# Attention's bias added by VectorE from broadcast rows, softmax factors applied where x is loaded

## The chip, the cores and the metric

One core of a Trainium2 chip runs the whole program. TensorE (PE) multiplies matrices, VectorE (DVE), ScalarE (ACT) and GpSimd (POOL) do the elementwise work, and SyncE (SP) issues the transfers, all of them on one queue. The metric is device time in microseconds, the median of three runs: 1035.31 us before (1035.18 to 1039.88).

## The reference

Attention of 4 batches, 8 heads, 576 tokens and head size 64, with a bias from running sums; then two feed-forward stages over 2304 tokens (width 512; 2048 and 1536 inner columns).

```python
scores = scale * q @ k.T                              # scale = 1/8
cum = np.cumsum(np.maximum(s, 0.0), axis=-1)
bias = -(cum[:, :, :, None] - cum[:, :, None, :])
scores = np.where(causal, -1e9, scores + np.minimum(bias, 0.0))
scores -= scores.max(-1, keepdims=True)
attn = np.exp(scores); attn /= attn.sum(-1, keepdims=True) + 1e-9
x = attn @ v                                          # heads side by side: (2304, 512)
h = x @ w_in; x = (h * np.cos(h)) @ w_out             # FF1, d_ff 2048
# FF2: rms norm, silu(x @ w_gate) * (x @ w_val) @ w_out, d_ff 1536
```

Within a row of scores the term of the query cancels in the softmax, so what a row needs is cum of the key, up to a constant.

## The kernel before

The kernel writes its operations into a list with costs and priorities; a planner then plays a list schedule on five engines and issues the instructions of each engine in the order it found. The times in it are its own; on the chip each engine follows that fixed order and waits on semaphores. Attention's steps get priorities one after the other, `P_ATT` (9000 ns) per pair of heads; a tick of FF1 (256 tokens by 256 inner columns) has priority `T_FF1` + 8094 ns times its number, so from 45 us on in the planner's time attention and FF1 are interleaved on every engine.

Attention runs over 16 pairs of heads (`Run`), four for each batch. A pair has two parts: "a" (query tiles 0 and 1) and "b" (tiles 2, 3 and "p", which puts both heads' last 64 queries into one tile). A unit of a part does the scores, the exponentials, and two units later (`DEPTH`) the transposes of the exponentials and the product with V (`av`); the order is a, then b with tile 2 and p, then b with tile 3.

The scores `score` and `score_p` come from fp32 matmuls of q and k (L515, L542). The bias is put on by a second matmul into the same PSUM bank: a column of ones and zeros (`pick`, `pk`) selects a head's row out of `ds`, where all heads' centred running sums lie in two float32r pieces (L520, L543). VectorE then adds a fixed causal mask (`cm`, `cp`), scales and takes the row's minimum (L527, L546); ScalarE takes the exponential and its row sum (L554). `norm` divides: GpSimd adds 1e-9 (L562), VectorE takes reciprocals (L564), and each of the pair's nine tiles of exponentials is multiplied by its column of reciprocals on ScalarE, VectorE or GpSimd, as the planner finds (L571, L570, L569). The transposes are L585, their copies out of PSUM L345 and L348, the product with V L617, and the result goes to `x_d` in DRAM. Attention uses PSUM banks 4 to 7.

FF1 loads a block of x from `x_d` (`load_x1`), splits it into two float32r pieces on ScalarE and VectorE (L345, L356) and multiplies (L724 and L730). Its weights come as 64-bit floats and are converted on the way (L436 to L443). Before the first pair, VectorE makes the running sums (L673, L675), centres them (L681) and writes the pieces of `ds` (L694).

## Time and profile before

| what | value |
|---|---|
| median of 3 runs | 1035.31 us |
| profiled execution, its own time | 1037.51 us |
| its span, first to last instruction | 1035.7 us |
| PE busy | 1016.1 us, 98% |
| VectorE, ScalarE, GpSimd busy | 74%, 58%, 9% |
| DMA | 206.04 MB, mean 199 GB/s |

The profile is of one execution. The busy time of PE counts from an instruction's start to an end that is modelled, and matmuls overlap: two that stream one behind the other are both counted as running. So what a matmul costs is read from the start of one to the start of the next. Attention's last product starts at 285.7 us; FF1 begins at 71.3 us.

### The profile page before, as it was taken

How to read it: one execution, taken by the hardware profiler on the slowest of the kernel's cores; microseconds unless marked ns; L12 is line 12 of the kernel's file. 1: busy time of each engine (PE TensorE's matmuls, PEld its weight loads, DVE VectorE, ACT ScalarE, POOL GpSimd, SP SyncE). 2: the span in 40 equal slices, each digit the busy share in tenths (PEclk: the TensorE clock that was granted, in tenths of full speed). 3: DMA queues.
4: the chain of work that ended last, by engine and by line, in shares of the span. 5: the costliest groups of instructions: out<-in, count | busy, mean ns of one | idle time of the engine just before them, and what ended most of it. 6: DMA issues, size and time to landing. Idle time of an engine off the chain costs nothing.

```text
span 1035.7 us, 19232 instructions
## 1 busy us (share of the span) xinstructions
PE 1016.1 (98%) x6738; PEld 911.3 (88%) x6738; DVE 769.4 (74%) x1804; ACT 596.4 (58%) x1268; POOL 94.9 (9%) x171
## 2 busy tenths in 40 slices
PE   7989999999999999999999999899999999999998
PEld 5667777777798999989899989899999999999998
DVE  7899999765446889888867795966566658987661
ACT  7989989998844766665554574311121125665440
POOL 1333353000000010110111000000000000000000
PEclk9999999999999999999999999999999999999999
DMA  6675786544394664666755545466373658997761
GB/s 209 208 249 190 232 276 194 169 140 131 97 355 163 219 244 172 242 227 202 249 176 183 169 132 179 137 204 199 119 235 116 221 175 243 299 327 216 222 194 42
DMA packets 143649, 206.04 MB, mean 199 GB/s; under 512 B 13760, under 2 KB 107456, under 8 KB 143552
## 3 DMA queue, kind: packets, MB, share of 16 engines
q1 hardware_dynamic: 143552, 204.81, 60.7%
q8 instruction: 53, 0.87, 0.4%
q14 instruction: 44, 0.36, 0.1%
HBM read 129.93 MB, written 74.84 MB: 198 GB/s over the span
## 4 chain that ended last, share of the span: by engine, by line
PE 78%; DVE 11%; ACT 4%; issue 3%; DMA 3%; POOL 1%; SPq 0%; DVEq 0%; POOLq 0%; ACTq 0%
PE bank L967 24%; PE bank L724 15%; PE bank L730 14%; PE bank L1108 13%; PE bank L585 3%; PE bank L617 3%; DVE wk L356 3%; PE bank L515 3%; DVE e L527 1%; DVE wk L441 1%; DVE wg L356 1%; ACT e L554 1%; DVE wk L443 1%; PE bank L542 1%; DMA wk<-in_w_gate_dram 1%
## 5 line engine op out<-in xcount | busy, mean ns | idle before, releaser
L356 DVE TENSOR_TENSOR wk<-wk,bank 128x384 f32<-128x384 f32 (+2 forms) x315 | 172.9, 554 | 151.7 <-PE bank L967 73.5
L724 PEld LDWEIGHTS bank<-xa,wi 128*128 128x128 f32 x1728 | 215.1, 188 | 9.4 <-DVE wk L356 2.4
L724 PE MATMUL bank<-xa,wi 128*128 128x256 f32 x1728 | 221.1, 283 | 1.6 <-DVE wk L356 1.3
L730 PE MATMUL bank<-wr,wg 128*128 128x512 f32 x672 | 166.0, 396 | 0.0
L730 PEld LDWEIGHTS bank<-wr,wg 128*128 128x128 f32 x672 | 122.6, 188 | 25.3 <-ACT wk L345 0.3
L967 PE MATMUL bank<-wi,wg 128*128 128x384 f32 x504 | 116.4, 340 | 3.3 <-ACT wk L345 2.9
L967 PE MATMUL bank<-wr,wg 128*128 128x384 f32 x504 | 116.7, 339 | 0.0
L345 ACT ACTIVATE wk<-bank 128x384 f32<-128x384 f32 (+2 forms) x79 | 39.5, 522 | 118.6 <-PE bank L967 79.0
L345 ACT ACTIVATE wg<-wk 128x512 fp32r<-128x512 f32 (+1 forms) x131 | 72.9, 573 | 57.8 <-DVE wk L356 47.5
L356 DVE TENSOR_TENSOR wg<-wk,wg 128x512 fp32r<-128x512 f32 (+1 forms) x148 | 90.9, 632 | 15.0 <-ACT wg L345 14.7
L967 PEld LDWEIGHTS bank<-wi,wg 128*128 128x128 f32 x504 | 90.3, 190 | 4.7 <-ACT wk L345 3.2
L356 DVE TENSOR_TENSOR wk<-wk 128x384 f32<-128x384 f32 (+1 forms) x198 | 91.3, 503 | 0.7
L967 PEld LDWEIGHTS bank<-wr,wg 128*128 128x128 f32 x504 | 91.7, 189 | 0.0
L440 POOL TENSOR_SCALAR wk<-wk 128x512 f32<-128x512 f32 x68 | 52.1, 769 | 301.4 <-ACT wk L437 258.8
L345 ACT ACTIVATE wr<-wr 128x384 fp32r<-128x384 f32 x115 | 58.2, 523 | 33.6 <-DMA wr<-g_S 13.1
L1108 PE MATMUL bank<-wi,wr 128*128 128x256 f32 x618 | 77.6, 281 | 0.0
L356 DVE TENSOR_TENSOR wk<-bank,wk 128x512 f32<-128x512 f32 (+1 forms) x90 | 59.2, 658 | 22.4 <-ACT wk L842 21.7
L1108 PEld LDWEIGHTS bank<-wi,wr 128*128 128x128 f32 x618 | 75.1, 188 | 0.0
L840 ACT ACTIVATE wk<-bank,quarter 128x512 int32<-128x512 f32 x72 | 49.1, 682 | 44.3 <-PE bank L724 43.2
L554 ACT ACTIVATE e<-e,mn 128x256 f32<-128x256 f32 (+3 forms) x128 | 70.7, 555 | 6.9 <-DVE mn L527 6.5
L842 ACT ACTIVATE wk<-wk,half_pi 128x512 f32<-128x512 f32 x72 | 52.1, 723 | 30.7 <-DVE wk L356 30.3
L527 DVE CUSTOM_DVE_ANT_0 e<-bank,cm 128x128 f32<-128x128 f32 (+3 forms) x128 | 56.8, 482 | 14.2 <-PE bank L520 11.7
(129 smaller groups left out, 1575.0 us busy)
## 6 DMA issues: line engine op xcount, KB each, us to landing
wk<-in_w_out_dram SPq DMA_DIRECT2D x28, 512.0 KB, 5.1
g_S<-wk SPq DMA_DIRECT2D x72, 192.0 KB, 3.1
wr<-g_S SPq DMA_DIRECT2D x56, 192.0 KB, 3.5
g<-wk SPq DMA_DIRECT2D x54, 192.0 KB, 2.4
wr<-g SPq DMA_DIRECT2D x50, 192.0 KB, 3.6
w_g<-wg SPq DMA_DIRECT2D x18, 512.0 KB, 3.6
w_v<-wg SPq DMA_DIRECT2D x18, 512.0 KB, 3.2
wk<-in_w_in_dram SPq DMA_DIRECT2D x16, 512.0 KB, 4.5
```

Source lines behind the costliest of these rows:

```text
L345: alts.append(("ACT", (act_p if psum else act_s)(n), lambda: act.activation(o(), i(), AF.Copy, scale=scale)))
L356: return plan.op(on("DVE", dve1(n), lambda: dve.tensor_tensor(out=o(), in0=a(), in1=b(), op=op)), r, w, **kw)
L440: plan.op(on("POOL", pool1(512), lambda: pool.tensor_scalar(out=top().bitcast(F32), in0=top().bitcast(F32), scalar1=0.0, scalar2=1.0, op0= ...
L515: pe.matmul(Sp[e]()[:, o:o + w], run.q()[hd, q0:q0 + 128], run.k()[hd, :w], start=(t == ts[0]), stop=False)
L527: plan.op(on("DVE", dve1(w) + 17, lambda o=o, w=w, i=i, e=e: dve.tensor_tensor_reduce(out=Es[e]()[:, o:o + w], in0=Sp[e]()[:, o:o + w], in ...
L554: plan.op(on("ACT", act_s(w) + 187, lambda E=E, o=o, w=w, i=i: act.activation(E()[:, o:o + w], E()[:, o:o + w], AF.Exp, scale=-1.0, bias=s ...
L724: pe.matmul(h, w[:, a, 128 * k:128 * k + 128], x[k // 2][:, k % 2, c, :blk], start=(n == 0), stop=(n == 11))
L730: pe.matmul(acc[t], g[a][:, 128 * t:128 * t + 128], w[:, c, :], start=(first and (a, c) == (0, 0)), stop=(last and (a, c) == (1, 0)))
L840: plan.op(on("ACT", act_p(512) + 93, lambda u=u, h=h: act.activation(u().bitcast(I32), h(), AF.Identity, bias=quarter)), [h], [u])
L842: plan.op(on("ACT", act_s(512) + 93, lambda u=u: act.activation(u(), u(), AF.Sin, scale=-TWO_PI, bias=half_pi)), [], [u], table="sin")
L967: pe.matmul(bank_()[:, :HALF2], G[i]()[:, u, o + 128 * k:o + 128 * k + 128], xs[k]()[:, c, :], start=(first and n == 0), stop=(n == 5), sk ...
L1108: pe.matmul(bk_()[:, col:col + 256], gs[p // 3]()[:, u, 128 * (p % 3):128 * (p % 3) + 128], w3[p][i]()[:, c, o:o + 256], start=(n == 0), s ...
```

## The change

- The matmuls that add the bias are gone, and with them `pick`, `pk`, `ds` and the fixed masks. The running sums of all 32 heads are made once, on 32 partitions, and stored to DRAM (`c_d`). For each pair four DMAs spread the two heads' rows over the partitions (`ce`, 128 partitions of 512 values for each head, and `cp`, 64 of 576 for each head). VectorE's instruction on the scores reads `ce` or `cp` where it read the mask.
- GpSimd puts the causal mask into these tiles (`masks`): tile 3, p and tile 0 when they have landed (tile 0 into a copy, `m0`), tile 2 after VectorE has read tile 3, tile 1 after tile 2. Therefore the units run in the order b with 3, b with 2 and p, a.
- For the first pair `first_bias` loads s itself, spread over the partitions, and VectorE makes the running sums there (`running`).
- `norm` is gone. `factors` takes a pair's nine row sums through a reciprocal, a PE transpose and a copy to DRAM (`rn_d`); `load_x1` loads them spread over partitions (`rb`) and multiplies x by them.
- The four pairs of the first batch take all eight PSUM banks. `P_ATT` is 8000.

```diff
-P_ATT, P_FF1, P_SET, P_OUT = 9000.0, 8093.98, 7350.0, 2145.0
+P_ATT, P_FF1, P_SET, P_OUT = 8000.0, 8093.98, 7350.0, 2145.0
...
+    ce_r, cp_r, m0_r = ring("ce", 2, [128, 2, 512], F32, "att"), ring("cp", 2, [128, S], F32, "att"), ring("m0", 2, [128, 2, 128], F32, "att")
+    rb_r = ring("rb", 1, [128, 2, BLK1], F32)
...
+            c, cp = self.ce, self.cp = ce_r.new(), cp_r.new()
+            if bp:
+                for e in range(2):
+                    h = 2 * bp + e
+                    load(lambda e=e: c()[:, e, :], lambda h=h: c_d()[h, 0:512].partition_broadcast(128), 1 << 18, [c_d], [(c, (t, e)) for t in range(4)])
+                    load(lambda e=e: cp()[64 * e:64 * e + 64, :], lambda h=h: c_d()[h, :].partition_broadcast(64), 256 * S, [c_d], [(cp, e)])
+            else:
+                first_bias(c, cp)
...
+                    plan.op(on("POOL", 360, lambda t=t, at=at: pool.affine_select(
+                        out=at() if t else self.m0(), in_=at(), pattern=[[0, 2], [-1, 128]], base=0, channel_multiplier=1,
+                        compare_op=ALU.is_ge, fill=-8.0 * BIG)), r, w)
...
+            return psb("first", (0, 1, 2, 3, 4, 5, 6, 7)) if self.bp < 4 else psb("att", (4, 5, 6, 7))
+
+        def factors(self):
+            rs, tr, rt = self.rs, self.bank(), rt_r.new()
+            dst = rn_d[self.bp]
+            plan.op(on("DVE", 130, lambda: dve.tensor_scalar(
+                out=rs(), in0=rs(), scalar1=1e-9, scalar2=float(2.0 * np.pi), op0=ALU.add, op1=ALU.mult)), [], [rs])
+            plan.op(on("DVE", 204, lambda: dve.reciprocal(out=rs(), in_=rs())), [], [rs])
+            plan.op(on("PE", 109, lambda: pe.transpose(tr()[:9, :128], rs(), ident)), [rs], [tr], rows=0.1)
+            copy(lambda: rt()[:9, :], lambda: tr()[:9, :128], 128, [tr], [rt], psum=True)
+            load(dst, lambda: rt()[:9, :], 4608, [rt], [dst])
...
-                        pe.matmul(Sp[e]()[:, o:o + w], pick[hd, e, self.bp:self.bp + 1].to_broadcast([64, 128]), ds()[hd, DS[t][0]:DS[t][0] + w], start=False, stop=(t == ts[-1]))
...
-                        out=Es[e]()[:, o:o + w], in0=Sp[e]()[:, o:o + w], in1=cm()[:, 512 - w:512], scale=-0.125, scalar=3.0e38,
+                        out=Es[e]()[:, o:o + w], in0=Sp[e]()[:, o:o + w], in1=run.ce()[:, e, :w] if t else run.m0()[:, e, :], scale=-0.125, scalar=3.0e38,
...
+                if t > 1:
+                    run.masks((t - 1,))
...
-                pe.matmul(Sp()[:, :288], run.pk(), ds()[:, o + gs.start:o + gs.stop], start=False, stop=True)
...
-                plan.op([
-                    ("POOL", 2.44 * w + 290, lambda at=at, by=by: pool.tensor_scalar(out=at(), in0=at(), scalar1=by(), scalar2=None, op0=ALU.mult)),
-                    ("DVE", 0.62 * w + 110, lambda at=at, by=by: dve.tensor_scalar(out=at(), in0=at(), scalar1=by(), scalar2=None, op0=ALU.mult)),
-                    ("ACT", act_s(w) + 93, lambda at=at, by=by: act.activation(at(), at(), AF.Copy, scale=by())),
-                ], [(rn, a)], [(E, part)])
...
-        us = [(p, u) for p in run.parts.values() for u in p.units()]
+        us = [(p, u) for c in "ba" for p in (run.parts[c],) for u in p.units()]
...
+                for k in (k0, k0 + 1):
+                    for e in range(2):
+                        o = 512 * e + t0 if t0 < 512 else 1024 + 64 * e + t0 - 512
+                        f = rn_d[b * NP + k]
+                        load(lambda rb=rb, e=e, k=k - k0, c0=c0, n=n: rb()[64 * e:64 * e + 64, k, c0:c0 + n],
+                             lambda f=f, o=o, n=n: f().rearrange("a b -> (a b)")[o:o + n].partition_broadcast(64), 256 * n, [f], [(rb, (k, e, c0))])
...
+            two(src, src, rb, 512, [rb], [raw], op=ALU.mult)
```

The change gives every engine a new order; three places show how. In these rows a number behind an underscore tells apart the buffers of one name.

PE, the first pair's scores before: q by k (L515 for tiles of one query block and both heads, L542 for p), and behind each its bias matmul (L520, L543).

```order
L515 MATMUL bank_123<-kr_127,qr_125 128x384
L515 MATMUL bank_124<-kr_127,qr_125 128x384
L520 MATMUL bank_123<-ds_133,pick 128x384
L520 MATMUL bank_124<-ds_133,pick 128x384
L542 MATMUL bank_121<-kr_127,qr_125 128x288
L543 MATMUL bank_121<-ds_133,pk_129 128x288
L542 MATMUL bank_122<-kr_127,qr_125 128x288
L543 MATMUL bank_122<-ds_133,pk_129 128x288
```

PE, the first pair's scores in the changed kernel (L537 and L561 are q by k).

```order
L537 MATMUL bank_98<-kr_108,qr_106 128x512
L537 MATMUL bank_99<-kr_108,qr_106 128x512
L537 MATMUL bank_100<-kr_108,qr_106 128x384
L537 MATMUL bank_101<-kr_108,qr_106 128x384
L561 MATMUL bank_102<-kr_108,qr_106 128x288
L561 MATMUL bank_103<-kr_108,qr_106 128x288
L537 MATMUL bank_105<-kr_108,qr_106 128x128
L537 MATMUL bank_98<-kr_108,qr_106 128x128
```

What was one group of matmuls and a bias group behind it is one group alone, the widest tile comes first, and all eight banks are used.

VectorE before its first scores, before the change: max (L673), running sum (L675), centring (L681), and the second piece of `ds` (L694).

```order
L681 TENSOR_SCALAR e_136<-ep_143 128x128
L681 TENSOR_SCALAR e_137<-ep_143 128x256
L673 TENSOR_SCALAR ep_142<-ep_142 128x320
L694 SCALAR_TENSOR_TENSOR ds_133<-e_136,halves,ds_133 128x128
L675 SCALAR_TENSOR_TENSOR ep_143<-ones,ep_143,ep_142 128x320
L694 SCALAR_TENSOR_TENSOR ds_133<-e_137,halves,ds_133 128x256
L681 TENSOR_SCALAR e_138<-ep_143 128x384
L681 TENSOR_SCALAR ep_142<-ep_143 128x576
L681 TENSOR_SCALAR e_140<-ep_143 128x512
L694 SCALAR_TENSOR_TENSOR ds_133<-e_138,halves,ds_133 128x384
L694 SCALAR_TENSOR_TENSOR ds_133<-ep_142,halves,ds_133 128x576
L527 ISA e_136,mn_151<-bank_121,cm_134 128x128
```

VectorE before its first scores in the changed kernel; the same steps are L668, L669, and L671 with L672. Four rows of the first head stand ahead of these.

```order
L669 SCALAR_TENSOR_TENSOR ce_112<-ones,e_123 128x512
L672 TENSOR_SCALAR ce_112<-ce_112,e_122 128x512
L671 COPY e_123<-ce_112 128x1
L668 TENSOR_SCALAR kr_109<-kr_109 128x576
L672 TENSOR_SCALAR ce_112<-ce_112,e_123 128x512
L669 SCALAR_TENSOR_TENSOR cp_114<-ones,kr_109 128x576
L668 TENSOR_SCALAR ep_124<-ep_124 32x576
L671 COPY kr_109<-cp_114 128x1
L669 SCALAR_TENSOR_TENSOR ep_125<-ones,ep_124 32x576
L672 TENSOR_SCALAR cp_114<-cp_114,kr_109 128x576
L671 COPY ep_124<-ep_125 32x1
L544 ISA e_122,mn_133<-bank_98,ce_112 128x512
```

The running sums are made three times over 128 partitions and once over 32 (`ep`), each over its full length, and stand ahead of the first score (L544); the pieces of `ds` are gone.

SyncE's queue around the loads of one of the first pairs, before (the queries `qr` and keys `kr` of a pair, its values `vr`, results to `x_d`, weights `wk` and `wo_d`).

```order
L359 DMA vr_131<-in_vp_dram 128x2x320
L359 DMA x_d_0b<-xu_145 128x320
L359 DMA qr_126<-in_q_dram 128x640
L359 DMA kr_128<-in_k_dram 128x576
L359 DMA x_d_1a<-xu_146 128x256
L359 DMA wk<-in_w_out_dram 128x1024
L359 DMA wk<-in_w_in_dram 128x1024
L359 DMA wk<-x_d_1a 128x256
```

The same place in the changed kernel (`ce` and `cp` are the spread bias, `rn_d` the factors, `rb` the factors spread for x).

```order
L343 DMA vr_111<-in_vp_dram 128x2x320
L343 DMA x_d_1a<-xu_126 128x256
L343 DMA rn_d_141<-rt_137 9x128
L343 DMA cp_114<-c_d 64x576
L343 DMA qr_106<-in_q_dram 128x640
L343 DMA kr_109<-in_k_dram 128x576
L343 DMA ce_112<-c_d 128x512 x2
L343 DMA cp_114<-c_d 64x576
L343 DMA wo_d_198<-wg 128x1024
L343 DMA wk<-in_w_out_dram 128x1024
L343 DMA wk<-x_d_1a 128x256
L343 DMA rb_138<-rn_d_141 64x256 x2
```

The queue has four bias loads for each pair, one store of factors, and two or more loads of factors ahead of each tile of x, between the instructions that were there.

## Rows read from the trace of the kernel before

**Rows 1.** The page, part 1: busy us of each engine, share of the span, instructions.

```profile
PE 1016.1 (98%) x6738; PEld 911.3 (88%) x6738; DVE 769.4 (74%) x1804; ACT 596.4 (58%) x1268; POOL 94.9 (9%) x171
```

**Rows 2.** Busy time by stretch: us, each engine's busy us (instructions), granted clock, DMA share, GB/s.

```profile
0.00:20.00 20.00, 15.12 (x79) 11.24 (x80) 14.62 (x63) 12.50 (x31) 3.78 (x19) 0.91 0.68 240
20.00:80.00 60.00, 56.28 (x402) 38.80 (x401) 53.66 (x168) 55.01 (x160) 17.90 (x34) 1.00 0.70 221
80.00:140.00 60.00, 59.82 (x423) 46.06 (x423) 56.61 (x148) 57.88 (x130) 21.56 (x36) 1.00 0.65 220
140.00:180.00 40.00, 37.48 (x262) 27.79 (x263) 37.56 (x95) 36.18 (x81) 18.90 (x27) 1.00 0.72 228
180.00:290.00 110.00, 109.89 (x795) 84.00 (x792) 68.32 (x225) 94.46 (x217) 5.15 (x22) 1.00 0.45 137
```

**Rows 3.** What PE waited for: us in total, times, longest us.

```profile
PE bank L585 <- DVE mn L527: 3.2, 3, 1.7
PE bank L542 <- DVE mn L527: 1.1, 1, 1.1
```

**Rows 4.** PE's timeline, 194 to 203 us: start, us, line, operation, tiles, shape, count.

```profile
194.02 0.65 PE L542 MATMUL bank<-kr,qr 128*128 128x288 f32 x2
194.29 0.51 PE L543 MATMUL bank<-ds,pk 128*128 128x288 f32 x1
194.64 1.60 PE L724 MATMUL bank<-xa,wi 128*128 128x256 f32 x12
196.07 0.60 PE L585 MATMUL bank<-ident,e 128*128 128x128 f32 x4
201.32 1.13 PE L515 MATMUL bank<-kr,qr 64*128 64x512 f32 x4
201.88 0.80 PE L520 MATMUL bank<-ds,pick 64*128 64x512 f32 x2
202.61 0.55 PE L585 MATMUL bank<-ident,e 128*128 128x128 f32 x3
```

**Rows 5.** Costliest groups: line, tiles, count | busy us, mean ns | idle before, releaser.

```profile
L571 ACT ACTIVATE e<-e,rn 128x384 f32<-128x384 f32 (+3 forms) x65 | 35.8, 576 | 3.3 <-DVE rn L564 2.8 <-DVE st L798 0.4
L571 ACT ACTIVATE ep<-ep,rn 128x576 f32<-128x576 f32 x7 | 5.4, 766 | 0.5 <-DVE rn L564 0.5
L570 DVE TENSOR_SCALAR e<-e,rn 128x256 f32<-128x256 f32 (+3 forms) x57 | 21.5, 405 | 1.0
L570 DVE TENSOR_SCALAR ep<-ep,rn 128x576 f32<-128x576 f32 x9 | 5.0, 556 | 0.1
L564 DVE RECIPROCAL rn<-rn 128x4 f32<-128x4 f32 (+2 forms) x48 | 8.1, 169 | 16.4 <-POOL rn L562 15.6
```

**Rows 6.** VectorE's timeline, first 20 us (columns as in Rows 4, idle in brackets).

```profile
3.87 0.69 DVE L675 TENSOR_TENSOR_SCAN ep<-ones,ep 128x256 f32<-128x256 f32 x1
5.62 0.88 DVE L675 TENSOR_TENSOR_SCAN ep<-ones,ep,ep 128x320 f32<-128x320 f32 x1
7.54 0.48 DVE L681 TENSOR_SCALAR e<-ep 128x512 f32<-128x512 f32 x1
9.29 0.28 DVE L527 CUSTOM_DVE_ANT_0 e<-bank,cm 128x128 f32<-128x128 f32 x1
18.10 0.42 DVE L348 COPY xu<-bank 128x256 f32<-128x256 f32 x1 [1.51 <-PE bank L617]
```

**Rows 7.** SyncE's queue: its waits to 290 us, then one issue of its timeline.

```profile
SPq L359 <- DVE wk L443: 41.7, 17, 5.9
4.04 0.88 SPq L359 DMA_DIRECT2D gbc<-in_rms_g_dram  x1
```

**Rows 8.** GpSimd: one group (columns as in Rows 5), and one line, ns min/median/max.

```profile
L701 POOL TENSOR_SCALAR_AFFINE_SELECT cm<-cm 128x128 f32<-128x128 f32 x1 | 0.3, 292 | 0.0
L562 POOL TENSOR_SCALAR rn<-rs x48: 192/195/737, 11.8 to 277.9; 128x4 f32<-128x4 f32 x16, 128x3 f32<-128x3 f32 x16, 128x2 f32<-128x2 f32 x16
```

**Rows 9.** VectorE's groups from 290 to 640 us (columns as in Rows 5).

```profile
L356 DVE TENSOR_TENSOR wk<-bank,wk 128x512 f32<-128x512 f32 x58 | 39.7, 685 | 17.6 <-ACT wk L842 17.3
```

176 lines of the change are left out of this document (77 added, 99 removed).

## Prediction

> **What bounds the kernel now.** I began with the page's busy times: PE is busy for 98% of the span, far ahead of VectorE and ScalarE [rows 1]. That points to PE, but it is an average, so I cut the span into stretches next [rows 2]. Attention lies in the first 290 us. From 180 to 290 us PE loses 0.11 us of 110 and ScalarE and VectorE have room: there only the work on PE counts. From 20 to 180 us three engines are nearly full at once: of 160 us PE is busy 153.6, VectorE 147.8, ScalarE 149.1. There PE stands idle 3.7 + 0.2 + 2.5 = 6.4 us, and in the first 20 us another 4.9. The list of waits says for whom: mostly for VectorE to have read the scores, so that a bank comes free or the next unit can go on [rows 3].
>
> The idle time is not all of it, since the end of a matmul is modelled. A second measure is the weight loads: their busy share is 76% from 180 to 290 us, where PE never waits, and 77% from 80 to 140, but 65% from 20 to 80 and 69% from 140 to 180 [rows 2]. At the density of the stretch without waits, the work of 20 to 80 us fits in 38.80 / 0.764 = 50.8 us and that of 140 to 180 in 36.4: 9.2 + 3.6 = 12.8 us of slack, twice the visible idle time. The Trainium skill (Trainium Kernel Development and Optimization, Performance Expectations) has this as a rule: matmul busy time is a bad measure of the distance to the roof, the weight loads' share a good one. By it the slack is 12.8 us, by the idle column 6.4; a rival below takes the larger figure.
>
> **The change part by part.**
>
> *Bias matmuls on PE.* They go: for each pair 2 x (128 + 256 + 384 + 512) columns, of which the two heads' run side by side, so 1280, and 2 x 288 for p; 1856 in all. From start to start, twelve float32r matmuls of 256 columns take 196.07 - 194.64 = 1.43 us, 0.465 ns a column [rows 4]. So the stream costs 0.86 us a pair and 13.8 us for 16 pairs. That is the low end. The high end reads the cost from the start of a bias group to the start of the next: 0.35 us for p, twice, and 0.73 us at width 512 [rows 4], by columns 1.10 us for the other three, 2.53 us a pair, 40 us. I take the value near the low end, because a start here is not the beginning of a stream: p's q-by-k pass has 4 x 288 columns' worth of work, 0.54 us at this rate, but the bias matmul is recorded 0.27 us behind it, so it queues behind it; the whole of 0.62 us is no more than the two streams together, 0.54 + 0.13. At width 512 the group takes 1.29 us against 0.95 + 0.24 = 1.19, so some 0.1 us of change-over is in it. Half of that for three widths makes 0.86 + 0.15 = 1.0 us a pair: 16 us.
>
> *The transpose of the factors.* One more for each pair. Three transposes or four start within 0.11 us of each other at best (four in 0.60 us with their tail) [rows 4]; with a change-over I take 0.2 us, between 0.1 and 0.6: 3.2 us (1.6 to 10). PE's work falls by 12.8 us.
>
> *The norms.* 144 multiplications of exponentials go: 35.8 + 5.4 = 41.2 us from ScalarE and 26.5 from VectorE, and with them 8.1 us of reciprocals [rows 5]. Added are two small instructions a pair on VectorE (0.17 us each by the reciprocals' row, 5.4 us) and one small copy on ScalarE (about as much). The multiplication of x is 18 times 128 x 512 at 0.685 us [rows 9], 12 us on VectorE, five of them before 290 us. Attention's exponentials, copies and scores stay. So over the first 290 us ScalarE loses some 36 us of work and VectorE some 26, far more than PE. What it is worth is PE's slack between 20 and 180 us: 0 to 12.8 us. I take half, 6.4 us: after the relief VectorE and ScalarE still carry the weights' conversion there, and a fixed order keeps some waits. The eight banks for the first batch belong here: the waits for VectorE to read scores [rows 3] are the ones they ease; FF1's banks among them are not asked for before x of the fourth pair, which comes later than the last use.
>
> *The beginning.* Before, the first score is read at 9.29 us [rows 6]. Now the running sums stand ahead of it, over full width. A scan costs 0.69 us at 256 columns and 0.88 at 320, so 2.9 ns a column: 1.44 us at 512, 1.63 at 576. Four scans, four maxima, three centrings at 0.48 to 0.52 and three or four small copies are 6.1 + 2.0 + 1.5 + 0.3 = 9.9 us, from about 3.5 us on: the first score at 13.4, 4.1 us later. But the scores then come without pauses, whereas before VectorE waits after its first scores (1.51 us before 18.10 alone [rows 6]), and three norms are gone from there; the second pair's bias has landed by then. I take 1.5 us, between -1 and +5. The granted clock was 0.91 on average in the first 20 us and 1.00 after [rows 2]; a second stretch at 1.2 GHz there is within that bound.
>
> *The transfers.* A pair's bias is 2 x 256 KiB and 2 x 64 x 2304 bytes, 0.82 MB. At 0.70 busy the DMA engines move 221 GB/s [rows 2], so 316 at most; 0.82 MB is 2.6 us of them for each pair. Five pairs' scores stand ahead of FF1's first matmul at 71.3 us, the first read at 9.29 [rows 6]: some 12 us a pair. So the DMA engines' share rises there from 0.70 to about 0.9; later it has room. The loads stand a pair ahead of their use, and behind them the queue holds the next weights and stores. SyncE issues a spread load in 0.88 us at worst [rows 7], 3.5 us a pair; it mostly waits. I cost them at nothing while the lead of one pair, ten microseconds, holds.
>
> *The product path of x.* The factors' round trip (copy, store, load, multiply) ends before the last blocks of attention on PE that stand ahead of FF1's first matmul: between the fourth pair's factors and that matmul lie some two pairs of work, over 20 us at 12 us a pair, against two transfers and three short instructions. Without that cover it would be one wait of about 10 us. Later blocks: nothing, VectorE is 62% busy from 180 us on [rows 2]; with no cover, 18 x 0.7 = 12 us.
>
> *Sum.* -16 + 3.2 - 6.4 + 1.5 = -17.7 us. The profiled execution took 1037.5 us (span 1035.7), 2.2 us more than the median of 1035.3; the sum gives 1019.8 for it and 1017.6 for the median. Forecast: 1018 us.
>
> **The rivals.**
>
> *All slack goes.* ScalarE and VectorE lose 36 and 26 us where they were full, and PE becomes the only bound from 20 us on, at the density of the later stretch. Then -12.8 - 12.8 and no loss at the beginning: -25.6, 1010 us. For it: the two engines were 92 to 96% busy. Against: the order is fixed, and the first 80 us still convert weights.
>
> *GpSimd's masks hold VectorE.* Now VectorE's scores of tile 2 wait for a mask that waits for the scores of tile 3, and tile 1 for tile 2; behind the waiting instruction stand VectorE's copies out of PSUM, for which PE waits. A mask of 128 x 128 is 0.29 us alone, yet a tiny GpSimd instruction takes from 0.19 to 0.74 us [rows 8], and in front of a mask there can be a weight conversion. At 0.6 us for each of 32, 19 us go from VectorE's 26 freed ones. PE's slack stays and some 5 us of new waits come: -12.8 + 1.5 + 5, 1029 us. Against: between two such scores VectorE has other instructions in its row. The Trainium skill (SBUF — State Buffer, "SBUF: two separate sides") says that VectorE and GpSimd share a port pair, and that in certain forms one of them blocks for the other's whole instruction; the spread from 0.19 to 0.74 us agrees with it. By it the masks, 0.29 us, would take up to 0.8.
>
> *Bias rows come late.* SyncE's queue is in order and stands behind other engines, up to 5.9 us at a time behind a weight conversion [rows 7]; 60 bias loads and the factors' stores and loads are put into it, and the DMA engines are near 0.9 in the first pairs. Where a pair's four loads come late, GpSimd's masks, VectorE's scores and all of PE's row behind them wait. From 17.7 / 15 = 1.2 us for each loaded pair the gain is gone; at 2 us it is +30 - 17.7 = +12.3, 1048 us. Against: the lead of ten microseconds, and DMA at 0.45 from 180 us on.
>
> **How the numbers follow.** Forecast (1012 to 1026 us): 0.52. All slack: 0.13. Masks: 0.17. Late rows: 0.14. Something else, with no net effect: 0.04. Half a per cent, 5.2 us, is about what a measurement can tell from no change. Faster by more (under 1030.1): 0.51 + 0.13 + 0.09 of the masks = 0.73. Slower by more: 0.13. Between: 0.14. The range 1006 to 1033 us leaves out the late rows and the far ends of the bias matmuls' cost. The forecast's own range is 1012 to 1026.
>
> **What would show it.** The bias matmuls right: from 180 us on, a pair with its ticks of FF1 takes about 0.8 us less of PE. The slack: from 20 to 180 us less PE idle time, a higher share of weight loads, and ScalarE and VectorE below 90%. The beginning: first score at 13 us, the second pair's scores by 26. The masks: waits of VectorE for GpSimd at the scores, over 0.3 us each. Late rows: GpSimd's masks waiting for DMA with VectorE idle behind them. Wrong I would be if PE's idle time before 290 us grows, or if FF1's first matmul stands waiting for x.

## The result and the profile after

| kernel | median | range | runs |
|---|---|---|---|
| before | 1035.41 us | 1034.80 to 1039.88 | 12 |
| changed | 1041.09 us | 1039.78 to 1043.37 | 12 |

The changed kernel takes 1.0054 times as long as the one before, with a 95% interval of 1.0043 to 1.0066. That is 5.7 us more, where 17.7 us less were forecast; 1041 us lies outside the range of 1006 to 1033.

PE's busy time fell, as meant, by 7.8 us of 1016.1 [rows 1], and it is still the busiest engine by far. The span of the profiled execution grew by 5.3 us all the same, so PE stands idle 13.1 us longer. Part 1 of the page of the changed kernel:

```profile
PE 1008.3 (97%) x6594; PEld 892.7 (86%) x6594; DVE 757.9 (73%) x1726; ACT 569.1 (55%) x1220; POOL 103.4 (10%) x178
```

Where does it go? Fixed stretches of time, as in [rows 2], compare different work, because the changed kernel is ahead of the other in one place and behind in another. So I cut at a piece of work: the first product of FF1's 17th tick. A tick is 24 products with `w_in` (L724 before, L710 after) and the 12 that follow with `w_out`; attention's products all stand among the first 16 of the 72 ticks, and the other 56 stand alone. This product in PE's timeline, before and then after (columns as in [rows 4]):

```profile
298.62 2.08 PE L724 MATMUL bank<-xa,wi 128*128 128x256 f32 x16
```

```profile
290.38 2.30 PE L710 MATMUL bank<-xa,wi 128*128 128x256 f32 x18
```

The stretches up to this product and from it to the last product of FF1, before (columns as in [rows 2]):

```profile
0.00:298.60 298.60, 287.19 (x2000) 215.50 (x2001) 234.56 (x699) 260.12 (x622) 67.28 (x135) 0.99 0.61 196
298.60:627.60 329.00, 327.72 (x2097) 296.30 (x2096) 259.81 (x533) 197.98 (x358) 27.62 (x36) 1.00 0.60 209
```

And after:

```profile
0.00:290.40 290.40, 274.77 (x1857) 196.89 (x1858) 216.41 (x609) 232.77 (x574) 76.02 (x142) 1.00 0.79 254
290.40:633.00 342.60, 332.46 (x2096) 296.04 (x2095) 266.74 (x546) 197.25 (x357) 27.43 (x36) 1.00 0.62 208
```

The reader sees two opposite changes. Up to the 17th tick the change gains 298.6 - 290.4 = 8.2 us. In the second stretch, where the change touches only the loading of x (and the order of instructions), the same 2096 matmuls take 342.6 instead of 329.0 us: 13.6 us are lost, 8.9 of them as visible idle time of PE (10.1 instead of 1.3), the rest inside busy times. What follows FF1 differs by 0.1 us. -8.2 + 13.6 - 0.1 = +5.3 us, the difference of the two profiled spans.

SyncE's queue in the middle of that stretch, in the changed kernel:

```profile
399.94 1.23 SPq L343 DMA_DIRECT2D w_g<-wg  x2
403.72 7.49 SPq L343 DMA_DIRECT2D rb<-rn_d  x12
411.31 0.53 SPq L343 DMA_DIRECT2D w_v<-wg  x1
411.88 1.27 SPq L343 DMA_DIRECT2D wk<-in_w_gate_dram  x2
```

Twelve loads of factors, for one of the two tiles in which a block of x comes, hold the queue for 7.5 us, and loads of weights for the second stage, `in_w_gate`, are issued behind them. What that leads to stands in the chain of waits of the same kernel (start, us, what):

```profile
412.36 9.84 DMA wk<-in_w_gate_dram
422.28 0.69 ACT wk L421
423.05 0.66 POOL wk L424
423.73 0.70 DVE wk L425
...
448.86 0.45 SPq L343
449.35 0.60 SPq L343
...
453.82 2.48 DMA rb<-rn_d
456.69 1.29 DVE wk L340 x2
...
459.82 0.64 ACT wg L329
460.50 4.79 PE bank L716 x12
```

Those weights come at 422 us, and their conversion on ScalarE, GpSimd and VectorE begins only then. (They took 9.84 us to land, where the loads of the same tensor took 3.7 to 7.0 us in the kernel before; what part of the lateness is the issue and what part the landing, no run separates.) From 448.86 us on SyncE itself is the path: it issues one factor load behind the other, about 0.6 us each, until the last one at 453.82. VectorE, which is bound to its order, multiplies x when they have landed, and only behind that and more instructions of its row comes the piece of h * cos(h) (in the tile `wg`) for which PE waits:

```profile
454.98 2.98 PE L710 MATMUL bank<-xa,wi 128*128 128x256 f32 x24
460.50 4.79 PE L716 MATMUL bank<-wr,wg 128*128 128x512 f32 x12 [2.54 <-ACT wg L329]
```

The twelve products behind this wait take 4.79 us; twelve others, behind a wait of 0.37 us at 409.02, take 3.07. The granted clock is 0.66 on average in these 5 us (columns as in [rows 2]), so part of them ran at 1.2 GHz, and about 1.7 us of the loss inside busy times lie here:

```profile
460.00:465.00 5.00, 4.50 (x12) 3.36 (x13) 5.00 (x12) 3.38 (x7) 0.00 (x0) 0.66 0.71 235
```

The waits from 290 to 640 us in the changed kernel (columns as in [rows 3]) list such events. In the kernel before, PE's idle time there, from the 17th tick on, is 1.3 us in all:

```profile
ACT wk L421 <- DMA wk<-in_w_gate_dram: 11.8, 5, 3.6
...
PE bank L716 <- ACT wg L329: 5.6, 5, 2.5
PE bank L710 <- DVE wk L340: 2.2, 4, 0.9
```

The stretches of attention, to be laid beside [rows 2]:

```profile
0.00:20.00 20.00, 13.81 (x62) 9.68 (x63) 14.77 (x43) 6.24 (x18) 4.52 (x16) 1.00 0.82 277
20.00:80.00 60.00, 53.15 (x365) 31.86 (x365) 50.13 (x148) 50.33 (x148) 24.08 (x45) 1.00 0.99 298
80.00:140.00 60.00, 58.78 (x413) 42.90 (x410) 50.40 (x134) 52.03 (x120) 19.88 (x31) 1.00 0.81 259
140.00:180.00 40.00, 39.42 (x262) 28.77 (x262) 36.22 (x96) 35.89 (x90) 13.72 (x23) 1.00 0.84 278
180.00:290.00 110.00, 109.22 (x762) 83.36 (x761) 64.59 (x190) 88.20 (x203) 13.81 (x28) 1.00 0.64 213
```

VectorE and ScalarE are relieved, yet PE stands idle 6.9 us from 20 to 80 us (3.7 before), where the DMA engines are now busy for 99%.

### The profile page after: what moved, and what is told of

It reads as the page before. It is cut to its first block, busy times and chain, and to the rows that moved or that the text cites. A ratio compares the mean times of both kernels' runs of the same rounds, so it can differ in the third digit from the quotient of the medians.

```text
span 1041.0 us, 19247 instructions
## 1 busy us (share of the span) xinstructions
PE 1008.3 (97%) x6594; PEld 892.7 (86%) x6594; DVE 757.9 (73%) x1726; ACT 569.1 (55%) x1220; POOL 103.4 (10%) x178
## 4 chain that ended last, share of the span: by engine, by line
PE 66%; DVE 14%; DMA 7%; ACT 5%; issue 4%; SPq 3%; POOL 1%; DVEq 0%; POOLq 0%; ACTq 0%
PE bank L967 25%; PE bank L1108 13%; PE bank L710 8%; PE bank L716 8%; DVE wk L340 5%; PE bank L587 4%; PE bank L619 3%; DMA wk<-in_w_gate_dram 3%; PE bank L537 3%; SPq L343 3%; DVE wg L340 2%; DVE wk L425 2%; DVE wk L427 1%; DMA wk<-in_w_out_dram 1%; PE bank L561 1%
## 5 line engine op out<-in xcount | busy, mean ns | idle before, releaser
L710 PE MATMUL bank<-xa,wi 128*128 128x256 f32 x1728 | 221.1, 282 | 2.3 <-DVE wk L340 2.2
L710 PEld LDWEIGHTS bank<-xa,wi 128*128 128x128 f32 x1728 | 213.8, 188 | 10.8 <-DVE wk L340 3.5
L716 PE MATMUL bank<-wr,wg 128*128 128x512 f32 x672 | 170.2, 401 | 7.9 <-ACT wg L329 5.6
L329 ACT ACTIVATE wk<-bank 128x512 f32<-128x512 f32 (+2 forms) x81 | 40.7, 523 | 115.8 <-PE bank L967 80.1
L572 ACT ACTIVATE e<-e,mn 128x128 f32<-128x128 f32 (+3 forms) x128 | 70.6, 555 | 16.5 <-DVE mn L544 16.3
L340 DVE TENSOR_TENSOR wk<-bank,wk 128x512 f32<-128x512 f32 (+1 forms) x90 | 59.3, 659 | 16.5 <-ACT wk L842 15.6
L840 ACT ACTIVATE wk<-bank,quarter 128x512 int32<-128x512 f32 x72 | 49.0, 680 | 36.3 <-PE bank L710 35.7
L425 DVE SCALAR_TENSOR_TENSOR wk<-wk 128x512 int32<-128x512 int32 x68 | 50.3, 741 | 24.8 <-POOL wk L424 24.7
```

Of the source, the lines that this page charges most:

```text
L329: alts.append(("ACT", (act_p if psum else act_s)(n), lambda: act.activation(o(), i(), AF.Copy, scale=scale)))
L340: return plan.op(on("DVE", dve1(n), lambda: dve.tensor_tensor(out=o(), in0=a(), in1=b(), op=op)), r, w, **kw)
L425: plan.op(on("DVE", dve1(512), lambda: dve.scalar_tensor_tensor(out=top(), in0=low(), scalar=29, in1=top(), op0=ALU.logical_shift_right, o ...
L572: plan.op(on("ACT", act_s(w) + 187, lambda E=E, o=o, w=w, i=i, c=c: act.activation(E()[:, o:o + w], E()[:, o:o + w], AF.Exp, scale=-1.0, b ...
L710: pe.matmul(h, w[:, a, 128 * k:128 * k + 128], x[k // 2][:, k % 2, c, :blk], start=(n == 0), stop=(n == 11))
L716: pe.matmul(acc[t], g[a][:, 128 * t:128 * t + 128], w[:, c, :], start=(first and (a, c) == (0, 0)), stop=(last and (a, c) == (1, 0)))
```

## The experiments

The theory after the comparison, called Q below: in FF1 the loads of the factors cost their time in SyncE's queue, which is in order. There are 120 of them, 84 in the stretch from the 17th tick on. Its rivals: the multiplication of x by the factors on VectorE, the traffic of the DMA engines, and losses that began in attention. The table gives each kernel's ratio to the one before on the same chip, when the 17th tick begins, and how long FF1 takes from there. The last two columns are read from one execution of each kernel, the medians from four to twelve, which lie up to 7 us apart (bias part alone: 1037.91 to 1045.11); a difference of 2 or 3 us in one of these columns is therefore not told apart from none.

| kernel | median us | ratio (95%) | 17th tick, us | FF1 from there, us |
|---|---|---|---|---|
| before | 1035.41 | | 298.6 | 329.0 |
| changed | 1041.09 | 1.0054 (1.0043-1.0066) | 290.4 | 342.6 |
| no factor loads | 1028.12 | 0.9924 (0.9907-0.9941) | 290.0 | 327.1 |
| bias loads for two pairs alone | 1042.82 | 1.0055 (1.0040-1.0070) | 288.1 | 341.0 |
| bias part alone | 1041.14 | 1.0047 (1.0030-1.0065) | 306.6 | 327.4 |
| factor part alone | 1046.18 | 1.0094 (1.0078-1.0109) | 294.5 | 342.4 |
| 60 factor loads | 1030.70 | 0.9947 (0.9932-0.9962) | 291.8 | 330.1 |
| before + 120 loads, unused | 1045.40 | 1.0098 (1.0081-1.0115) | 303.6 | 328.9 |
| before + 120 loads, waited for | 1044.09 | 1.0080 (1.0065-1.0095) | 297.3 | 337.4 |
| four banks | 1051.44 | 1.0155 (1.0136-1.0174) | 299.4 | 343.7 |
| no masks | 1039.45 | 1.0037 (1.0023-1.0052) | 288.0 | 341.5 |
| no sums | 1040.73 | 1.0049 (1.0034-1.0064) | 289.7 | 341.7 |
| no sums, q and k first | 1042.59 | 1.0075 (1.0058-1.0092) | 291.3 | 340.9 |
| factors on attention's result | 1158.51 | 1.1181 (1.1164-1.1198) | 417.8 | 332.1 |
| the same, one-row loads | 1055.69 | 1.0198 (1.0183-1.0214) | 317.0 | 328.0 |
| 60 factor loads, bias merged | 1065.64 | 1.0288 (1.0272-1.0303) | 326.6 | 328.7 |
| 60 factor loads, wide bias merged | 1029.76 | 0.9937 (0.9919-0.9956) | 291.1 | 327.9 |

**No factor loads.**

```diff
-    rb_r = ring("rb", 1, [128, 2, BLK1], F32)
+    rb = ring("rb", 1, [128, 2, BLK1], F32).new()
+    plan.op([("POOL", 600, lambda: pool.memset(rb(), 1.0))], [], [rb])
...
-                        load(lambda rb=rb, ...: rb()[64 * e:64 * e + 64, k, c0:c0 + n], ...)
```

> The changed kernel without the loads of the factors for x: x is multiplied by a tile of ones that is set once (so the output lacks the softmax's division); the factors are still made and stored. Measure: FF1's stretch from the first matmul of its 17th tick to its last matmul, 329.0 us before the change (298.6 to 627.6) and 342.6 us after (290.4 to 633.0). Theory Q (SyncE's queue: 120 spread loads at 0.59 us keep the gate weights' loads back, and their conversions hold ScalarE and VectorE): the stretch falls back to 329 to 332 us, total 1027 to 1031 us. Rival V (the multiplication itself, 18 times 0.69 us on VectorE ahead of FF1's chain): the stretch stays at 338 us or more, total 1036 us or more.

Without the loads the stretch takes 327.1 us, with the multiplication still there. So the multiplication by itself costs nothing, and the loads, or the waits for them, cost the 13.6 us and more. The stretch, columns as before:

```profile
290.00:617.10 327.10, 325.83 (x2097) 295.04 (x2096) 265.48 (x544) 199.06 (x359) 30.05 (x36) 1.00 0.61 210
```

**Bias loads for two pairs alone** (later pairs use these rows again).

```diff
-            c, cp = self.ce, self.cp = ce_r.new(), cp_r.new()
-            if bp:
+            c, cp = self.ce, self.cp = (ce_r.new(), cp_r.new()) if bp < 3 else (runs[bp - 2].ce, runs[bp - 2].cp)
+            if bp > 2:
+                pass
+            elif bp:
```

> The changed kernel with the bias rows loaded for pairs 1 and 2 only; later pairs read the tiles of the pair two before (so the bias of 13 pairs is wrong), and all masks, scores and factor loads stay. 52 of 60 bias loads and 10.6 MB are gone. Theory D (bias rows fill the DMA engines, 0.99 busy from 20 to 80 us, and the work waits for transfers): the 17th tick of FF1 begins at 279 to 285 us instead of 290.4, FF1's first matmul at 70 to 78 us instead of 89.4; FF1's loss of 13 us stays; total 1030 to 1036 us. Rival M (the chain score, mask, score between VectorE and GpSimd, or the head): the 17th tick begins at 288 to 292 us, total 1038 to 1042 us.

```profile
20.00:80.00 60.00, 53.34 (x369) 31.96 (x366) 53.14 (x155) 48.87 (x146) 23.85 (x47) 1.00 0.84 263
```

The DMA engines are no longer full from 20 to 80 us (0.84), yet PE is busy there as long as in the changed kernel. FF1's first product does come earlier, at 79.8 instead of 89.4 us, but the 17th tick only by 2.3 us, and the time is the same, much as the rival had it. The bias rows' traffic is not where the gain went.

**Each part alone.** The bias part keeps the norms of attention; the factor part is put on the kernel before.

```diff
 # bias part alone: the changed kernel, with norm() and without factors() and rb
+            queue.append(lambda part=part, keys=keys: part.norm(keys))
 # factor part alone: the kernel before, with
-            queue.append(lambda part=part, keys=keys: part.norm(keys))
+                load(lambda rb=rb, ...: rb()[64 * e:64 * e + 64, k, c0:c0 + n], ...)
+            two(src, src, rb, 512, [rb], [raw], op=ALU.mult)
```

> The bias part alone: bias rows by DMA and by VectorE, eight banks for the first batch, but the norms stay in attention as before the change, and x is not multiplied. Theories D and Q: FF1's stretch is 329 to 332 us as before the change; DMA is over 0.9 busy from 20 to 80 us; ScalarE and VectorE get no relief there, so the 17th tick begins no earlier than 296 us; total 1033 to 1042 us. If the masks' chain were the matter (M), the stretch is the same, but VectorE waits for GpSimd at the scores for more than 5 us in all, and the total is above 1042 us.

> The factor part alone: bias by matmul as before the change, row sums' factors multiply x when it is loaded, 120 spread loads. Theory Q: attention gains from the relief of ScalarE and VectorE without the bias rows' transfers, the 17th tick begins at 287 to 295 us; FF1's stretch is 339 to 343 us as after the change; total 1034 to 1041 us. Rival V says the same of FF1; rb_none tells them apart. If FF1's stretch here is 332 us or less, the loss in FF1 comes from the order and not from the factors' loads.

The stretches of the bias part alone, then of the factor part alone:

```profile
0.00:306.60 306.60, 281.90 (x1841) 200.03 (x1842) 235.10 (x676) 259.53 (x634) 94.73 (x201) 0.97 0.72 232
306.60:634.00 327.40, 326.13 (x2097) 295.19 (x2096) 259.72 (x533) 197.71 (x358) 27.09 (x36) 1.00 0.61 210
```

```profile
0.00:294.50 294.50, 285.08 (x2017) 212.00 (x2018) 210.07 (x618) 238.81 (x580) 43.14 (x72) 1.00 0.63 206
294.50:636.90 342.40, 332.50 (x2096) 297.11 (x2095) 267.84 (x546) 197.57 (x357) 27.95 (x36) 1.00 0.62 209
```

The loss in FF1 belongs wholly to the factor part (342.4 against 327.4). Up to the 17th tick the two parts don't add up: +8.0 and -4.1 us alone, -8.2 together. With the norms still there, PE's saved matmuls turn into idle time (306.6 - 281.9 = 24.7 us, 15.6 with both parts; the profiled execution of the bias part took 1044.16 us, its median is 1041.14); so the norms must go for the bias part to pay. The factor part alone came out above the time expected of it (1046.18 us, 1034 to 1041), with both stretches as expected.

**60 factor loads.** One transfer brings both pairs that a block needs; the same bytes, the same multiplication.

```diff
-                for k in (k0, k0 + 1):
-                    for e in range(2):
-                        load(... rb()[64 * e:64 * e + 64, k, c0:c0 + n], ... f()...[o:o + n].partition_broadcast(64) ...)
+                for e in range(2):
+                    load(... rb()[64 * e:64 * e + 64, :, c0:c0 + n],
+                         ... bass.AP(rn_d().tensor, ..., [[0, 64], [1152, 2], [1, n]]) ...)
```

> The changed kernel with the factors of a block of x fetched by half as many loads (60 instead of 120): one transfer brings both pairs that a block needs. The same bytes land in the same tile and the multiplication stays. Theory Q (the loss in the first feed-forward stage is SyncE's in-order queue, by the number of transfers it issues): the stretch from the 17th tick's first product to the stage's last one was 342.6 us with 120 loads and 327.1 with none, so about 333 to 337 with 60 if the queue's time goes by loads, and the time about 1032 to 1036. Theory B (it goes by bytes or rows moved, 64 rows of 1 KB or so for each pair): the stretch stays at 340 to 343 and the time at 1039 to 1042.

330.1 us: 12.5 of the 13.6 us are back, more than the half that was expected, and the kernel is 0.5% faster than the one before:

```profile
291.80:621.90 330.10, 328.79 (x2096) 295.43 (x2096) 266.25 (x545) 197.04 (x358) 27.67 (x36) 1.00 0.64 217
```

The bytes and what waits for them are the same, the number of loads is not. The order of instructions is a new one too, as in every kernel here, but the table speaks against it as the cause: the seven kernels with 120 factor loads that attention must make first take 340.9 to 343.7 us, the three with 60 take 327.9 to 330.1, and the six with none in FF1 327.1 to 332.1. ScalarE's waits for the gate and value weights of the second stage go the same way: 1.7 us in all before, 13.9 in the changed kernel, 5.5 with 60 loads, 3.2 with none. The factor loads as the trace lists them (ns min/median/max, first and last start), in the changed kernel and in this one:

```profile
L343 SPq DMA_DIRECT2D rb<-rn_d x120: 444/594/1697, 35.7 to 545.0; - x120
```

```profile
L343 SPq DMA_DIRECT2D rb<-rn_d x60: 573/605/1757, 48.8 to 530.6; - x60
```

A load of twice the bytes takes SyncE as long: 120 x 0.594 = 71 us of its queue became 60 x 0.605 = 36 us.

**The loads alone, on the kernel before.** First with nothing that reads them, then with the conversion of x made to wait.

```diff
+                        load(lambda rb=rb, ...: rb()[64 * e:64 * e + 64, k, c0:c0 + n],
+                             lambda ...: s[h, t0:t0 + n].partition_broadcast(64), 256 * n, [], [(rb, (k, e, c0))])
 # second run only
-            copy(lambda x=x: x()[:, :, 0, :], src, 512, [raw], [x])
+            copy(lambda x=x: x()[:, :, 0, :], src, 512, [raw, rb], [x])
```

> The kernel before, with nothing of the change but 120 spread loads of the same shape as the factors' (64 rows of up to 1 KB, from the bias rows in memory), issued at the same place for each block of x into a tile that nothing reads. Theory Q (SyncE's queue is what the loads cost): the stretch from the 17th tick's first product to the first feed-forward stage's last one grows from 329.0 us to 338 to 344, and the time from 1035 to 1044 to 1050, with no multiplication and no change in attention. Rival W (what costs is VectorE's wait for the factors, ahead of the conversion of x): nothing waits for these loads, so the stretch stays within 2 us of 329.0 and the time at 1034 to 1038.

> The kernel before with 120 spread loads of the factors' shape, and with the conversion of x made to wait for them; there is no multiplication and attention is unchanged. Without the wait (the run before this) the same loads were issued during attention, and the feed-forward stretch stayed at 328.8 us. Theory Q (what costs is 120 loads in SyncE's queue at the time when the stage's weights are due): the stretch is 337 us or more, the time 1044 to 1052. Rival R (the loads cost only because each must go through memory after attention's factors are known, and constant rows can be fetched whenever the queue is free): the stretch is 328 to 332 us, and the time 1036 to 1046, depending on what the loads take from attention.

The first run missed its aim: with nothing to wait for, the planner put the loads into attention's time (none of them is issued after the 17th tick), where they cost 5.0 us in the profiled execution, and FF1 was untouched. (By the medians the kernel takes 10 us longer; the profiled execution took 1043.19 us. Where the rest lies, its trace does not show.) In the second run 87 of them are issued in FF1, and the stretch grows by 8.4 us, with no multiplication and with attention as before:

```profile
297.30:634.70 337.40, 330.89 (x2096) 298.71 (x2095) 258.97 (x534) 197.65 (x357) 27.03 (x36) 0.99 0.63 213
```

Most of the 8.4 us come from one place. SyncE issues ten of the added loads, and behind them a load of weights, `in_w_val`:

```profile
361.33 6.88 SPq L359 DMA_DIRECT2D rb<-in_s_dram  x10
368.31 0.53 SPq L359 DMA_DIRECT2D w_g<-wg  x1
368.89 1.20 SPq L359 DMA_DIRECT2D wk<-in_w_val_dram  x2
```

These weights land at 376.4 us. ScalarE, which has their conversion next in its row, comes late to the step of FF1 behind it, VectorE waits for ScalarE, and PE for VectorE:

```profile
378.56 5.49 PE L725 MATMUL bank<-xa,wi 128*128 128x256 f32 x24 [4.44 <-DVE wk L356]
```

```profile
380.00:385.00 5.00, 5.00 (x23) 4.79 (x23) 4.96 (x11) 2.87 (x6) 0.00 (x0) 0.54 0.14 55
```

The wait is 4.44 us, and the 24 products behind it take 5.49 instead of the 3.00 us of the 24 at 387.00: the granted clock is 0.54 from 380 to 385 us, that is, nearly all of it at 1.2 GHz. So loads of this number at this place are enough to hold weights back and PE up, without a multiplication. How the 13.6 us of the changed kernel divide between this and VectorE's own waits for the factors (6.1 us there, from the 17th tick on) was not separated: there they are a dozen shorter waits, and the two sums can't be subtracted from each other.

**Four banks** for the first batch, as before the change.

```diff
-            return psb("first", (0, 1, 2, 3, 4, 5, 6, 7)) if self.bp < 4 else psb("att", (4, 5, 6, 7))
+            return psb("att", (4, 5, 6, 7))
```

> The changed kernel with four PSUM banks for the first batch's attention, as the kernel before has them; bias and factors stay changed. If the eight banks earn what they showed at the beginning (pairs 1 to 3 take 11.5 us each against 13 to 15 before), the first three pairs take 14 to 15 us each, the fifth pair begins at 64 us or later instead of 59.0, the 17th tick comes 4 to 6 us later (294 to 297) and the time is 1045 to 1047. Rival (what the first batch gains is lost in the wait that follows for weights and conversions): the 17th tick stays at 289 to 292 and the time at 1039 to 1043.

The 17th tick comes 9.0 us later, more than expected, and 6.3 us are lost within the first pair, whose first product with its values comes at 27.8 instead of 21.5 us; between the medians lie 10.3 us. (What the expectation calls the fifth pair's beginning is this product of the fourth pair: 70.5 instead of 59.0 us.) The first 20 us:

```profile
0.00:20.00 20.00, 13.95 (x54) 9.74 (x55) 13.37 (x40) 7.14 (x17) 5.20 (x17) 0.74 0.71 242
```

PE got through 54 matmuls there instead of 62, at a mean granted clock of 0.74 instead of 1.00, that is, with a longer part at 1.2 GHz. What of the 9.0 us is waiting for banks and what the clock that came with it, is not separated, and this is one execution, of 1054.26 us. In it the change without the eight banks gains nothing in attention (299.4 against 298.6 us before); I had seen in them only an easing of waits.

**What holds attention.** Three runs leave work out or change an order.

```diff
 # no masks (tile 0 then reads ce and not its copy m0)
-            for t in ts:
+            for t in ():
 # no sums: the rows of s themselves go to ce and cp
-            running(lambda e=e: c()[:, e, :], sb[e], 512, 128, [sb[e]], [(c, (t, e)) for t in range(4)], **kw)
 # no sums, q and k first: the same, and
-        kw = dict(prio=-5e5)
+        kw = dict(prio=0)
```

> The changed kernel with the causal masking of the bias rows by GpSimd left out (output is then not the reference's). Theory M (after the first pairs, attention's ticks wait on the masks, which GpSimd works off in order behind weight conversions): the 17th tick comes 5 us or more earlier than the 290.4 us of the changed kernel, at 280 to 285, and the time falls to about 1031 to 1036. Rival N (what holds attention is the sum of softmax and conversion work on VectorE and ScalarE with four PSUM banks): 288 to 291, and 1039 to 1042.

> The changed kernel with the running sums of the bias left out (the raw rows are spread over the partitions and added; output is then not the reference's). Theory H (the beginning costs the changed kernel 4 to 5 us, because the first score waits for the running sums on VectorE and their rows): the first product of the feed-forward stage and the 17th tick come 4 to 5 us earlier, at 285 to 287, and the time is about 1036 to 1037. Rival (the time at the beginning is made up by the next pairs): the 17th tick stays at 289 to 291 and the time at 1039 to 1042.

> The changed kernel with the running sums of the bias left out (output is then not the reference's), as in an earlier run, and with the first pair's queries and keys loaded ahead of the bias rows instead of behind them. If the order of the loads is what the beginning costs: the first score's addition on VectorE starts 1.5 us or more before the 11.5 us of the earlier run, the second pair's products at 33 to 35 us instead of 38.0, and the 17th tick comes 2 to 4 us before that run's 289.7. Rival (what is won at the beginning is waited for later, at the weights' conversion): the second pair comes earlier and the 17th tick stays at 288 to 291.

The masks are worth 2.4 us at the 17th tick in these executions (1.6 between the medians, whose intervals overlap), the sums nothing. In the third run VectorE's first score starts at 9.01 us (12.55 in the changed kernel, 11.49 without the sums alone), the fourth pair's first product with its values comes 2.5 us earlier (56.5 us), and the 17th tick is where it was, 291.3 us: what the beginning gives is waited away later, among the first ticks of FF1. None of the three is what holds attention back; where the rest of its missing gain is, stays open.

**Factors on attention's result**, so that x needs none, with one load of both heads' factors for each pair; then with two loads of one row.

```diff
+            two(lambda: xu()[:, :n], lambda: xu()[:, :n], lambda: rp()[:, lo:lo + n], n, [rp], [xu], op=ALU.mult)
 # first run: two rows in one load, for the factors and for both kinds of bias rows
+            load(rp, lambda: bass.AP(dst().tensor, dst().offset, [[S, 2], [0, 64], [1, S]]), 512 * S, [dst], [rp])
 # second run
+            for e in range(2):
+                load(lambda e=e: rp()[64 * e:64 * e + 64, :], lambda e=e: dst()[e, :].partition_broadcast(64), ...)
```

> The changed kernel with the factors multiplied into attention's result before it goes to memory, so that x needs no factors when it is loaded: one spread load for each pair (16 in all) in place of 120 in the feed-forward stage, and two multiplications of 256 and 320 columns for each pair; the bias rows of a pair come with two loads instead of four. Theory Q: the stage's stretch is then as without loads, 326 to 328 us, attention ends about where it does in the changed kernel (17th tick at 288 to 293), and the time is 1025 to 1030, faster than both kernels. Rival (the multiplication and its wait for the factor's round trip through memory hold the attention's store back): the 17th tick comes at 296 or later and the time is 1033 or more.

> The changed kernel with the factors multiplied into attention's result before it goes to memory, as in the run that came out at 1158 us, but every spread load is of one row to 64 or 128 partitions (two loads a pair for the factors, four for the bias rows) instead of two rows in one load. If it was the loads of two rows that made that run slow: the feed-forward stretch is 327 to 332 us, the 17th tick at 290 to 296, the time 1027 to 1035. If it was the round trip of the factors through memory ahead of attention's store, with one tile for them: the 17th tick comes after 320 us and the time is above 1060.

FF1 is fast in both (332.1 and 328.0 us), once more without factor loads in it, but attention stands behind the factors' way through memory. VectorE sat idle for the two-row loads 77.4 us in all. With loads of one row 100 us come back. The 317.0 us lie between what was expected of the two causes: PE's longest waits in attention are now for ScalarE's copy of a pair's factors into the one tile `rp` (columns as in [rows 3]), and the rest of its 35.7 us of idle time up to the 17th tick is in shorter waits:

```profile
PE bank L540 <- ACT rp L329: 12.4, 3, 10.2
```


**Bias rows merged too**, with 60 factor loads: first both kinds, then only the wide ones, whose pattern begins with the 128 partitions.

```diff
 # both runs
+                load(lambda: c(), lambda: bass.AP(..., [[0, 128], [S, 2], [1, 512]]), ...)
 # first run only
+                load(lambda: cp(), lambda: bass.AP(..., [[S, 2], [0, 64], [1, S]]), ...)
```

> The changed kernel with both kinds of spread loads merged: the factors of both pairs of a block in one transfer (60 in place of 120), and both heads' bias rows in one (2 loads a pair in place of 4). Theory Q: the feed-forward stretch is as with merged factors alone (329 to 332 us); in attention SyncE is not what ends the waits, so the bias loads add 0 to 2 us: 17th tick at 289 to 292, time 1028 to 1031, faster than both kernels. Rival (attention waits for SyncE's queue too, with 60 bias loads in it): 17th tick at 284 to 288, time 1024 to 1027.

> The changed kernel with merged factor loads (60), and with the wide bias rows of both heads in one load (its access pattern begins with the 128 partitions), while the narrow rows of p keep a load for each head. In the run with both kinds of bias loads merged, which came out at 1065.6 us, the merged load of the narrow rows began with the two heads. The Trainium skill (DMA: Bandwidth & Descriptors, Why a DMA increments its semaphore by 16 and not by 1) says that a load is spread over as many DMA engines, up to 16, as divide the outermost size of its pattern. If the two heads outermost are what made that run slow, GpSimd's longest wait for the narrow rows is as in the changed kernel again, the 17th tick at 289 to 293 and the time 1028 to 1032, faster than both kernels. If merging the bias rows itself is harmful (a longer load, one buffer for two heads), the 17th tick comes after 300 us and the time is above 1040.

The idle time ahead of the instructions that use the narrow rows `cp` (us in all, times), as far as its loading ended it, for the first run and then the second:

```profile
  DMA cp<-c_d: 57.4, 12
```

```profile
  DMA cp<-c_d: 8.0, 6
```

The merged narrow load, issued in 0.5 us like the others, comes so late that GpSimd, which masks the rows, waits 57.4 us for it (16.6 in the changed kernel); merging the wide rows costs nothing. The second run is the fastest of those that compute the whole result, 1029.76 us, 0.9937 of before (0.9919 to 0.9956), though not told apart from the one with 60 factor loads and separate bias loads. Its FF1:

```profile
291.10:619.00 327.90, 327.25 (x2097) 295.31 (x2096) 266.01 (x545) 197.69 (x358) 28.35 (x36) 1.00 0.64 217
```

## Why the prediction was wrong

The step that failed is *The transfers*: "it mostly waits. I cost them at nothing", and with it "Later blocks: nothing" of the product path of x. I counted the bias loads, five pairs of them, and looked for trouble at their place. The factor loads I named, in the round trip of x and in a rival, but neither counted nor priced them, nor did I ask what stands behind them in SyncE's queue: up to twelve at a time ahead of weights. That is 13.6 us. The price stood in the same paragraph, 0.88 us for a spread load (which is not the worst: the factor loads took 0.594 us in the median, up to 1.70); times 120 it would have shown 106 us of SyncE's time (71 by the median). SyncE waits indeed, but for other engines and at times that they set [rows 7], so not all of its waiting is time that the queue can give away: the 84 loads of FF1's second stretch are 50 us of issuing at 0.594 us each, much of it went into such waits, and still 13.6 us were lost.

A second term failed, *the slack*, by some 9 us; what took its place stays open for the most part (below).

Point by point:

- *Bias matmuls and transposes*: -12.8 us of PE's work were forecast; PE's busy time up to the 17th tick fell by 287.19 - 274.77 = 12.4, which agrees.
- *The slack*: -6.4 us forecast, none came. Apart from the beginning, PE's idle time up to the 17th tick grew, from 6.5 to 9.4 us. ScalarE and VectorE were relieved in the direction that was meant (27.4 and 18.2 us, forecast 36 and 26), and both fell below 90% from 20 to 180 us, yet the waits did not go. The relief is not worth nothing: the factor part alone has 2.0 us less of PE's idle time than the kernel before (9.4 instead of 11.4), and the bias part without it 24.7 us. But in the whole change other waits stand in their place, and of these the runs name only the masks and the bias rows, some 2 us each, which is no more than executions differ by. That PE's idle time before 290 us grows was one of the signs of being wrong that I had named, and it came. By the Trainium skill (Trainium Kernel Development and Optimization, Performance Expectations) the weight loads' share shows the distance to the roof; from 20 to 80 us it fell from 65 to 53%, which agrees with the grown idle time. The share shows slack, but not that the relief of another engine will fill it.
- *The beginning*: +1.5 us of idle time forecast, 1.3 measured (20 - 13.81 against 20 - 15.12); the first score was forecast at 13.4 us and came at 12.55. Close, but in part by luck: the 20 us hold other work than before, and the clock there was 1.00 instead of 0.91. The time of the first score turned out not to matter at the 17th tick.
- *The eight banks* were put down to the slack. Alone they are worth 9.0 us at the 17th tick (one execution each), more than the whole gain of 8.2 us there.
- *The product path of x*: FF1's first product moved from 71.3 to 89.4 us, but not for the factors: PE has no wait for x in attention, and the bias part alone, without factors, has it at 89.2.
- *The sum*: the difference of 23.0 us between -17.7 and +5.3 is 13.6 us in FF1 and 9.1 of idle time in attention (+4.2 instead of -6.4 + 1.5), the rest 0.3 us.
- *Rivals*: "Bias rows come late" named the mechanism, the queue in order, and its sign, but with the bias rows in attention; GpSimd does wait 16.6 us there for the narrow ones, yet without most of these loads only 2.3 us come back. "Masks hold VectorE" was put at 11 us, and without the masks 2.4 come back. "All slack goes" was wrong as the slack was.

## What to carry to other kernels

Count the transfers that an edit adds, not only their bytes, multiply by the time that the queue takes to issue one, and place each group in its queue: ask what is queued behind it and when that is due, in later stages too. Where a small operand must come from memory in pieces, shape its copy there so that few loads fetch it: half the loads turned a loss of 0.5% into a gain of 0.5%. Work taken from engines that are nearly full gained here only what the next thing in order let through, so cost it at little until a wait is named that will end sooner.

## What was not expected of the hardware

A spread load of 64 rows took SyncE 0.594 us to issue, and one of twice the bytes 0.605 us; the DMA engines were at 0.62 in the stretch where this cost 13.6 us.

A load whose pattern begins with two rows is slow to land: one issued at 39.02 us was used by GpSimd, which had waited for it, at 51.63, while the one-row loads in the changed kernel landed in 5.0 us (median). The Trainium skill (DMA: Bandwidth & Descriptors, Why a DMA increments its semaphore by 16 and not by 1) says that a transfer is spread over as many DMA engines, up to 16, as divide the outermost size of both its patterns; for two rows that is two. The runs agree: 57.4 us of waits with the two heads outermost, 8.0 without. How many engines moved it no row here shows. A sum of waits alone would not do as a sign: in the run with the factors on attention's result and one-row loads GpSimd waits 38.6 us for rows that land in 4.7 us (median).

A wait of PE can cost more than its length. Behind the 4.44 us at 374 us in the run with 120 loads waited for, the granted clock was 0.54 for 5 us, and the next 24 products took 2.5 us longer than others.
